# Two leftover output tiles taken as a pair through seven half products, and the ending's order dealt anew

## The chip, the cores and the metric

The kernel runs on one core of a Trainium2 chip. A core has several engines with instruction queues of their own: TensorE (PE; its weight loads are the row PEld) multiplies matrices into PSUM, VectorE (DVE) and ScalarE (ACT) read PSUM and write on-chip memory (SBUF), GpSimd (POOL) here mostly issues loads, and SyncE (SP) issues the stores and the DMA transposes. Sixteen DMA engines move the data. The metric is the device time of one execution in microseconds.

## The reference

Inputs are q, k, v of shape (8, 12, 448, 64) and four weights. Cut to what matters:

```python
scores = q @ k.T / sqrt(64) - log(448)          # per batch and head
x = sigmoid(scores) @ v                          # -> (8, 448, 768), heads side by side
h = relu(x.T @ w_tok1) @ w_tok2                  # mixing over tokens, 448 -> 256 -> 448
u = x + h.T
out = u + relu(u @ w_ch1) @ w_ch2                # mixing over channels, 768 -> 1536 -> 768
```

Output is (8, 448, 768) in float32. The kernel computes in float16 with float32 sums in PSUM.

## The kernel before, in words

One batch is a lot (0 to 7). A lot has three units of four heads each. The work of a unit is a cycle: `qk` (scores and sigmoid, seven pieces), `av` (product with v, result in xT), a DMA transpose to xn (`xtrans_dma`), `tok1` (first token product, ReLU on ScalarE into h1), `ytrans` (second token product, added to xT by VectorE, giving ut). A lot then goes through the channel mixing: `utrans` transposes u by DMA into un, `sevens` computes the hidden layer h2 (448 tokens x 1536), and the second product turns h2 into output rows in tiles of 128 tokens: tiles 0, 1 and 2, and a last piece of 64.

Two of the products use the seven-multiplication scheme of Strassen and Winograd in place of eight. `sevens` does so for the first channel product (L499 is its matmul), with `token_sums` making sums of ut halves on VectorE ahead of it. `ch2_seven` does so for the second product of tiles 0 and 1 of a lot: the two tiles are the two block rows, the low and high half of the 1536 hidden columns the block columns. A half product (`plain`, matmul L763) is six matmuls of 128x128 by 128x384. `sums` makes four sums of h2 blocks on VectorE (L751), and `end` adds each product's PSUM result to the output tile (L781). Products 1, 6, 7, 4 accumulate in one bank (chain X); 2 is chain Y; 5 and 3 are chain Z:

```python
CHAIN = {1: "X", 6: "X", 7: "X", 4: "X", 2: "Y", 5: "Z", 3: "Z"}
```

Tile 2 has no partner and takes the plain way, `ch2` (L549): two halves of 384 output columns, twelve matmuls each. The last 64 tokens of lot 6 go through `last_split` (L631) and those of lot 7 through `ch2_last` (L802, L813).

The order is written out by hand: each engine runs its instructions in the order in which the program names them, and a queue does not go past an instruction that waits. PSUM has eight banks: four named `m0` to `m3` (chosen with `at_bank`) and two tiles of two banks each with the tag `qk`, which the scores use and, in the ending, `av`, `last_split` and `sevens`. `at_bank[0] = Y` with Y = 0, and X = 2.

The ending comes after the loop over cycles: the last `av` and the last transposes of lot 7, the second product of lot 6 laid between them so that TensorE has work while the transposes, ReLUs and sums of lot 7 go on, then `sevens(7)`, then lot 7's second product and its last piece. `store` issues two DMAs per tile on SP (L585). The last piece is copied and stored by VectorE with SP and by ScalarE with its own queue (L823, L825, L834).

Of the kernel before, what the change touches and what calls it, by code (L numbers as in the profile page):

```python
# [9 lines left out]
FP16 = mybir.dt.float16  # L10
# [13 lines left out]
NU = 3  # L24
# [6 lines left out]
def kernel(  # L31
# [53 lines left out]
    def bank(shape, dtype, name):  # L85

        if opening_banks:
            n = opening_banks.pop(0)
        else:
            n = at_bank[0]  # L90
            at_bank[0] = (n + 1) % 4
        return pp.tile(shape, dtype, tag=f"m{n}", bufs=1, name=name)
# [146 lines left out]
    def xtrans_dma(b, u):  # L239
        nc.sync.dma_start_transpose(  # L240
            out=xn_tile(b, u).rearrange("s g t d -> s (g t) d"),
            in_=xTs[b % 2][:, u, :, :].rearrange("d g s -> d (g s)"),
        )
# [38 lines left out]
    def tok1(b, u, relu_on_vector=False, with_scores=False):  # L282

        if not with_scores:
            h1_tile(b, u)
            one = bank([128, 2, 2, 128], FP32, f"tk_{b}_{u}")
            tks[b] = [one[:, tcb, :, :] for tcb in range(2)]
        ps = tks[b]
        for tcb in range(2):
            cols = slice(128 * tcb, 128 * tcb + 128)  # L290
            for t in range(3 if with_scores else 4):
                rows = slice(0, 64 if t == 3 and N_FIRST <= NU * b + u < N_CYCLES - 2 else 128)
                nc.tensor.matmul(  # L293
                    out=ps[tcb],
                    lhsT=w1[rows, t, cols],
                    rhs=xn[b, u][rows, :, t, :],
                    start=(t == 0 and not with_scores),
                    stop=(t == (2 if with_scores else 3)),
                )
        for tcb in range(2):  # L300
            dst, src = h1[b, u][:, tcb, :, :], ps[tcb]
            if relu_on_vector:
                nc.vector.tensor_scalar(
                    out=dst, in0=src, scalar1=0.0, scalar2=None, op0=MAX
                )
            else:
                nc.scalar.activation(out=dst, in_=src, func=RELU)  # L307

    def ytrans(b, u, banks=()):
        for g in range(2):  # L310
            db = NU * g + u
            if banks:
                at_bank[0] = banks[g]
            ps = bank([128, 512], FP32, f"yt_{b}_{db}")
            for tcb in range(2):
                nc.tensor.matmul(  # L316
                    out=ps[:, 0:S],
                    lhsT=h1[b, u][:, tcb, g, :],
                    rhs=w2[:, tcb, :, :],
                    start=(tcb == 0),  # L320
                    stop=(tcb == 1),
                )
            nc.vector.tensor_tensor(  # L323
                out=uts[b % 2][:, db, 0:S], in0=xTs[b % 2][:, u, g, 0:S], in1=ps[:, 0:S], op=ADD
            )


    def utrans(b):
        if b < B - 1:
            nc.vector.tensor_copy(  # L330
                out=uts[b % 2][:, 0:NU, S:512], in_=uts[b % 2][:, NU:NDB, S - 64 : S]
            )
        un[b] = pa.tile([128, NDB, 4, 128], FP16, tag="un", bufs=2, name=f"un_{b}")
        nc.sync.dma_start_transpose(
            out=un[b].rearrange("s db t d -> s (db t) d"),
            in_=uts[b % 2].rearrange("d db s -> d (db s)"),
        )
# [203 lines left out]
    def ch2(b, t, half, n0=0, n1=NCB):  # L541
        cols = slice(DH * half, DH * half + DH)
        if n0 == 0:
            if half == 0:
                outs[b, t] = pa.tile([128, D], FP32, tag="outs", bufs=3, name=f"o_{b}_{t}")
            acc[b] = bank([128, 512], FP32, f"c2_{b}_{t}_{half}")
        ps = acc[b]
        for cb in range(n0, n1):
            nc.tensor.matmul(  # L549
                out=ps[:, 0:DH],  # L550
                lhsT=h2[b][:, BY_GROUP[cb], 128 * t : 128 * t + 128],
                rhs=c2[:, BY_GROUP[cb], cols],
                start=(cb == 0),
                stop=(cb == NCB - 1 and b in un),
            )
        if n1 < NCB:
            return
        if b not in un:
            for n in range(NU):
                nc.tensor.matmul(  # L560
                    out=ps[:, 128 * n : 128 * n + 128],
                    lhsT=uts[b % 2][:, NU * half + n, 128 * t : 128 * t + 128],
                    rhs=ident[:, :],
                    start=False,
                    stop=(n == NU - 1),
                )
        ch2_out(b, t, half, ps)
# [147 lines left out]
    class ch2_seven:  # L715

        CHAIN = {1: "X", 6: "X", 7: "X", 4: "X", 2: "Y", 5: "Z", 3: "Z"}

        def __init__(self, b, X, Y, Z):
            self.b, self.ps, self.banks = b, {}, {"X": X, "Y": Y, "Z": Z}  # L720
            hid = pa.tile(
                [128, 3, NCB // 2, 128], FP16, tag="tr_k", bufs=2, name=f"hid_{b}"
            )
            hid3 = pa.tile([128, NCB // 2, 128], FP16, tag="tr_q", bufs=2, name=f"hid3_{b}")
            self.held = {n: hid[:, at, :, :] for at, n in enumerate((5, 6, 7))}
            self.held[3] = hid3[:, :, :]
            h = h2[b]
            t0, t1 = slice(0, 128), slice(128, 256)
            self.a11, self.a12 = h[:, LOW, t0], h[:, HIGH, t0]
            self.a21, self.a22 = h[:, LOW, t1], h[:, HIGH, t1]  # L730
            self.weights = {1: self.a11, 2: self.a12, 4: self.a22}
            self.moving = {
                1: c2[:, LOW, D1],
                2: c2[:, HIGH, D1],
                3: c2[:, HIGH, D2],
                5: hsums[0],
                6: hsums[1],
                7: hsums[2],
                4: hsums[3],
            }  # L740
# [12 lines left out]
        def begin(self, n):  # L753
            chain = self.CHAIN[n]
            if n in (1, 2, 5):
                at_bank[0] = self.banks[chain]
                self.ps[chain] = bank([128, 512], FP32, f"c8_{self.b}_{n}")
            return self.ps[chain]

        def plain(self, n, k0=0, k1=NCB // 2):  # L760
# [11 lines left out]
                self.end(n)  # L772

        def end(self, n):
            b = self.b
            t, half = {1: (0, 0), 2: (0, 0), 6: (0, 1), 3: (0, 1)}.get(n, (1, int(n != 4)))
            if (b, t) not in outs:
                outs[b, t] = pa.tile([128, D], FP32, tag="outs", bufs=3, name=f"o_{b}_{t}")
            o = outs[b, t][:, DH * half : DH * half + DH].rearrange("s (u d) -> s u d", d=128)
            opens = n in (1, 6, 5, 4)  # L780
            nc.vector.tensor_tensor(  # L781
                out=o,
                in0=un[b][:, NU * half : NU * half + NU, t, :] if opens else o,
                in1=self.ps[self.CHAIN[n]][:, 0:DH].rearrange("s (u d) -> s u d", d=128),
                op=ADD,
            )
            if n in (3, 4):
                store(b, t)
# [485 lines left out]

    lot = B - 2
    before, ahead = divmod(N_CYCLES - 1, NU), divmod(N_CYCLES - 2, NU)
    seven = ch2_seven(lot, X, X + 1, X + 1)
    av(*before, banks=two_banks("xa_end"))
    steps, last_end = last_split(lot, two_banks("c2_end"))
    for f in steps:  # L1280
        f()
    seven.sums(0, 2)

    def halves(b, t, half):
        return [lambda n=n: ch2(b, t, half, n, n + 6) for n in (0, 6)]

    first, second = halves(lot, 2, 0), halves(lot, 2, 1)
    xtrans_dma(*before)
    seven.plain(1)
    seven.plain(2)  # L1290
    seven.sums(2, 4)
    seven.plain(6)
    seven.plain(5)
    last_end()
    at_bank[0] = Y
    tok1(*ahead)
    seven.plain(7)
    seven.plain(3)
    at_bank[0] = Y
    ytrans(*ahead)  # L1300
    token_sums(B - 1, 0, 2)
    seven.plain(4)
    at_bank[0] = X + 1
    first[0]()
    at_bank[0] = Y
    tok1(*before)
    first[1]()
    at_bank[0] = Y
    ytrans(*before)
    at_bank[0] = X  # L1310
    second[0]()
    second[1]()
    token_sums(B - 1, 2, NU)
    utrans(B - 1)
    sevens(B - 1)
    seven = ch2_seven(B - 1, Y + 1, Y, X)
    first, second = halves(B - 1, 2, 0), halves(B - 1, 2, 1)
    seven.plain(1)
    seven.sums(0, 4)
    seven.plain(2)  # L1320
    at_bank[0] = X + 1
    for f in first:
        f()
    seven.plain(5)
    seven.plain(6)
    at_bank[0] = Y
    second[0]()
    seven.plain(3)
    seven.plain(7)
    second[1]()  # L1330
    seven.plain(4)
    at_bank[0] = X
    for w, f in pieces_last(B - 1):
        f()

# [29 lines left out]
```

## Time and profile before

| | us |
|---|---|
| median of 3 runs | 345.11 (344.12 to 345.49) |
| the profiled execution | 343.85 |
| its span, first to last instruction | 341.9 |
| TensorE busy | 334.7 (98%) |
| VectorE busy | 216.7 (63%) |
| ScalarE busy | 212.5 (62%) |
| last TensorE work ends, from the span's start | 337.6 |

Times inside a profile are counted from the span's start. A row of the chain of work or of the timeline gives a start, a length, an engine, a line of the kernel, the tensors (output, then inputs) and a count. SPq and ACTq are the instruction queues that issue DMAs. In a group's row, the numbers after the bar are busy time and mean nanoseconds of one, then the idle time ahead of it and what ended that.

### The profile page before, as it was taken

To read this page: it belongs to the slowest core of one execution; us is meant where nothing else is said; L and a number is where in the kernel's file an instruction comes from. 1 tells how busy PE (TensorE), PEld (TensorE's weight loads), DVE (VectorE), ACT (ScalarE), POOL (GpSimd) and SP (SyncE) were. 2 spreads that over 40 slices of the span, in tenths; PEclk is the share of its full clock that TensorE was granted. 3 is DMA by queue.
4 is the path that set the end of the run, shared out by engine and by line. 5 is a ranking of instruction groups with operands and counts; after the bars stand their busy time and mean duration, and the time that the engine had idled before them with its cause. 6 is when DMAs were issued, how large, how long until landed. Compare 5 with 4: busy or idle time off the path is not lost.

```text
span 341.9 us, 10439 instructions
## 1 busy us (share of the span) xinstructions
PE 334.7 (98%) x4549; PEld 238.8 (70%) x4549; DVE 216.7 (63%) x438; ACT 212.5 (62%) x271; POOL 56.6 (17%) x98
## 2 busy tenths in 40 slices
PE   7999999999999999999999999999999999999994
PEld 4655566555886679766886679766896669768952
DVE  3376467588674775566574584666765685886662
ACT  4996846588658684877648785777648885102400
POOL 8992440040040004000130004000100000000000
PEclk9999999999999999999999999999999999999999
DMA  7999999999999799999999599948991438035406
GB/s 125 172 180 191 207 204 200 169 175 223 219 172 208 119 175 175 209 168 134 191 188 167 123 196 184 223 98 149 199 157 33 102 78 141 5 69 130 86 0 161
DMA packets 104380, 52.17 MB, mean 153 GB/s; under 512 B 76432, under 2 KB 101264, under 8 KB 104336
## 3 DMA queue, kind: packets, MB, share of 16 engines
q1 hardware_dynamic: 78944, 29.70, 47.8%
q0 software_dynamic: 25168, 21.50, 41.7%
q8 instruction: 35, 0.57, 0.7%
q10 hardware_dynamic: 224, 0.33, 0.3%
q14 instruction: 9, 0.07, 0.1%
HBM read 43.45 MB, written 11.01 MB: 159 GB/s over the span
## 4 chain that ended last, share of the span: by engine, by line
PE 90%; ACT 5%; DMA 1%; DVE 1%; issue 1%; ACTq 0%; DVEq 0%
PE c_ab L499 14%; PE qk L184 10%; PE c L549 9%; PE c_c L499 8%; PE c L375 8%; PE xa L215 8%; PE c L631 6%; PE tk L293 5%; PE yt L316 5%; ACT att L191 5%; PE c L763 4%; PE c L613 4%; PE c L352 3%; DMA first_q<-in_q_dram 1%; PE c L802 1%; PE c_a L499 1%
## 5 line engine op out<-in xcount | busy, mean ns | idle before, releaser
L191 ACT ACTIVATE att<-qk,att_bias 128x896 f16<-128x896 f32 x168 | 157.0, 1015 | 41.5 <-PE qk L184 41.1
L184 PE MATMUL qk<-tr_q,tr_k 64*64 64x448 f16 x672 | 57.5, 356 | 0.5 <-DVE tr_k L176 0.2
L499 PEld LDWEIGHTS <-c 128*128 128x128 f16 x504 | 48.4, 98 | 1.1 <-issue 0.3
L224 DVE CAST xT<-xa 128x448 f16<-128x448 f32 x46 | 26.6, 620 | 29.8 <-PE xa L215 29.8
L215 PE MATMUL xa<-att,raw_v 64*64 64x448 f16 x644 | 38.0, 349 | 0.0
L499 PEld LDWEIGHTS <-sum 128*128 128x128 f16 x378 | 36.3, 98 | 0.0
L184 PEld LDWEIGHTS <-tr_k 64*64 64x64 f16 x672 | 20.3, 105 | 19.7 <-issue 12.0
L572 DVE TENSOR_TENSOR o<-un,c 128x384 f32<-128x384 f16 x34 | 18.8, 554 | 23.3 <-PE c L613 10.2
L549 PE MATMUL c<-c,h 128*128 128x384 f16 x180 | 32.9, 326 | 0.0
L375 PE MATMUL c<-c,h 64*64 64x384 f16 x640 | 31.1, 322 | 0.0
L520 ACT ACTIVATE pt_ab<-c_ab 128x896 f32<-128x896 f32 x21 | 19.3, 917 | 16.9 <-PE c_ab L499 16.3
L323 DVE TENSOR_TENSOR ut<-xT,yt 128x448 f16<-128x448 f16 x48 | 27.5, 614 | 1.9 <-PE yt L316 1.9
L215 PEld LDWEIGHTS <-raw_v 64*64 64x64 f16 x672 | 20.3, 107 | 10.9 <-issue 0.4
L1039 POOL COPY gate<-tr_q 128x2 f16<-128x2 f16 x6 | 1.2, 195 | 154.0 <-DMA tr_q<-rel_q 154.0
L549 PEld LDWEIGHTS <-h 128*128 128x128 f16 x180 | 17.2, 98 | 11.3 <-issue 1.0
L307 ACT ACTIVATE h<-tk 128x256 f16<-128x256 f32 x42 | 14.2, 405 | 16.7 <-PE tk L293 16.7
L375 PEld LDWEIGHTS <-h 64*64 64x64 f16 x640 | 18.7, 107 | 7.9
L316 PE MATMUL yt<-w,h 128*128 128x448 f16 x96 | 22.1, 353 | 0.0
L631 PE MATMUL c<-c,h 64*64 64x384 f16 x480 | 22.1, 322 | 0.0
L522 ACT ACTIVATE h<-c_ab 128x896 f16<-128x896 f32 x7 | 6.4, 917 | 24.4 <-PE c_ab L499 24.4
L293 PE MATMUL tk<-xn,w 128*128 128x256 f16 x156 | 21.2, 274 | 0.1
L529 DVE TENSOR_TENSOR h<-pt_ab,c_ab 128x896 f16<-128x896 f32 x14 | 15.2, 1084 | 9.4 <-PE c_ab L499 9.4
(110 smaller groups left out, 473.3 us busy)
## 6 DMA issues: line engine op xcount, KB each, us to landing
out_dram<-o SPq DMA_DIRECT2D x48, 192.0 KB, 3.5
c<-in_moe_w_ch_dram POOLq DMA_DIRECT2D x4, 1152.0 KB, 15.6
raw_k<-in_k_dram POOLq DMA_DIRECT2D x10, 336.0 KB, 9.3
raw_q<-in_q_dram POOLq DMA_DIRECT2D x10, 336.0 KB, 13.3
raw_v<-in_v_dram POOLq DMA_DIRECT2D x10, 336.0 KB, 10.8
out_dram<-o SPq DMA_DIRECT2D x15, 96.0 KB, 2.2
raw_q<-in_q_dram POOLq DMA_DIRECT2D x12, 112.0 KB, 4.9
raw_k<-in_k_dram POOLq DMA_DIRECT2D x12, 112.0 KB, 4.8
```

The lines of the kernel that those rows point to most:

```text
L184: nc.tensor.matmul(out=ps[64 * g : 64 * g + 64, hi, 0:S], lhsT=tr[b, "k"][64 * hi : 64 * hi + 64, u, j, 64 * g : 64 * g + 64], rhs=tr[b, " ...
L191: nc.scalar.activation(out=att[b, u, j][:, :, :], in_=ps[:, :, 0:S], func=SIGMOID, bias=bias_t[:, :], scale=att_scale,)
L215: nc.tensor.matmul(out=ps[g][64 * hi : 64 * hi + 64, 0:S], lhsT=raw[b, "v"][64 * g : 64 * g + 64, u, hi, j, :], rhs=att[b, u, j][64 * g : ...
L224: nc.vector.tensor_copy(out=xTs[b % 2][:, u, g, 0:S], in_=ps[g][:, 0:S])
L293: nc.tensor.matmul(out=ps[tcb], lhsT=w1[rows, t, cols], rhs=xn[b, u][rows, :, t, :], start=(t == 0 and not with_scores), stop=(t == (2 if ...
L316: nc.tensor.matmul(out=ps[:, 0:S], lhsT=h1[b, u][:, tcb, g, :], rhs=w2[:, tcb, :, :], start=(tcb == 0), stop=(tcb == 1),)
L323: nc.vector.tensor_tensor(out=uts[b % 2][:, db, 0:S], in0=xTs[b % 2][:, u, g, 0:S], in1=ps[:, 0:S], op=ADD)
L375: nc.tensor.matmul(out=ps[p][m : m + 64, 0:n], lhsT=lhsT(p, part, m), rhs=rhs(p, part), start=(first and turn == 0), stop=(last and turn = ...
L499: nc.tensor.matmul(out=ps[:, g, p, :], lhsT=weights[n][:, d, 128 * cb : 128 * cb + 128], rhs=moving[n][:, d, :], start=(n in (1, 5, 2) and ...
L520: nc.scalar.activation(out=shaped(part[:, :, :]), in_=ps, func=COPYF)
L549: nc.tensor.matmul(out=ps[:, 0:DH], lhsT=h2[b][:, BY_GROUP[cb], 128 * t : 128 * t + 128], rhs=c2[:, BY_GROUP[cb], cols], start=(cb == 0), ...
L631: nc.tensor.matmul(out=ps[r][m : m + 64, 0:DH], lhsT=lhsT(part, n, m), rhs=rhs(part, n, m), start=(n == 0), stop=(n == n_cb - 1),)
```

## The change

Tile 2 of lot 6 and tile 2 of lot 7 become the two block rows of one more `ch2_seven`, named `both`. Lot 6's hidden layer is in a buffer that `sevens(7)` overwrites, so ScalarE copies its tile 2 to a buffer of its own (`held`) early in the ending. `ch2_seven` takes its rows and its h2 blocks as arguments. The output tile of lot 7's tile 2 goes to a buffer that held v, as the three output buffers are in use. In `both` and in lot 7's `seven`, chains Y and Z share a bank.

`ytrans` in the ending gets a two-bank tile and issues its four matmuls together, then its two adds. The order ahead of `sevens(7)` is dealt anew: `last_end` and both `tok1` come earlier, `token_sums` is done whole, `utrans` comes right behind the second `ytrans`. Behind `sevens(7)` the products of `both` and of `seven` alternate.

```diff
-    def ytrans(b, u, banks=()):
-        for g in range(2):
-            db = NU * g + u
-            if banks:
-                at_bank[0] = banks[g]
-            ps = bank([128, 512], FP32, f"yt_{b}_{db}")
+    def ytrans(b, u, banks=None):
+        def products(g, ps):
             for tcb in range(2):
                 nc.tensor.matmul(
...
+        def add(g, ps):
+            db = NU * g + u
             nc.vector.tensor_tensor(
                 out=uts[b % 2][:, db, 0:S], in0=xTs[b % 2][:, u, g, 0:S], in1=ps[:, 0:S], op=ADD
             )
+        for g in range(2):
+            ps = banks[g] if banks else bank([128, 512], FP32, f"yt_{b}_{NU * g + u}")
+            products(g, ps)
+            if not banks:
+                add(g, ps)
+        for g in range(2 if banks else 0):
+            add(g, banks[g])
...
-        def __init__(self, b, X, Y, Z):
-            self.b, self.ps, self.banks = b, {}, {"X": X, "Y": Y, "Z": Z}
+        def __init__(self, rows, sides, X, Y, Z):
+            self.rows, self.ps, self.banks = rows, {}, {"X": X, "Y": Y, "Z": Z}
...
-            h = h2[b]
-            t0, t1 = slice(0, 128), slice(128, 256)
-            self.a11, self.a12 = h[:, LOW, t0], h[:, HIGH, t0]
-            self.a21, self.a22 = h[:, LOW, t1], h[:, HIGH, t1]
+            (self.a11, self.a12), (self.a21, self.a22) = [
+                (side[:, LOW, :], side[:, HIGH, :]) for side in sides
+            ]
...
-    seven = ch2_seven(lot, X, X + 1, X + 1)
+    seven = ch2_seven(
+        [(lot, 0), (lot, 1)], [tokens(h2[lot], t) for t in range(2)], X, X + 1, X + 1
+    )
     av(*before, banks=two_banks("xa_end"))
     steps, last_end = last_split(lot, two_banks("c2_end"))
     for f in steps:
         f()
+    held = pa.tile([128, NCB, 128], FP16, tag="raw_v", bufs=2, name="held")
+    nc.scalar.activation(out=held[:, :, :], in_=tokens(h2[lot], 2), func=COPYF)
     seven.sums(0, 2)
...
-    first, second = halves(lot, 2, 0), halves(lot, 2, 1)
     xtrans_dma(*before)
+    last_end()
     seven.plain(1)
     seven.plain(2)
     seven.sums(2, 4)
+    at_bank[0] = Y
+    tok1(*ahead)
+    seven.plain(6)
+    at_bank[0] = Y + 1
+    tok1(*before)
+    ytrans(*ahead, banks=two_banks("yt_end_1"))
+    seven.plain(5)
+    ytrans(*before, banks=two_banks("yt_end_2"))
+    utrans(B - 1)
+    seven.plain(7)
+    token_sums(B - 1)
+    seven.plain(3)
+    seven.plain(4)
+    sevens(B - 1)
+    outs[B - 1, 2] = pa.tile([128, D], FP32, tag="raw_v", bufs=2, name=f"o_{B - 1}_2")
+    both = ch2_seven(
+        [(lot, 2), (B - 1, 2)], [held, tokens(h2[B - 1], 2)], Y, Y + 1, Y + 1
+    )
+    seven = ch2_seven(
+        [(B - 1, 0), (B - 1, 1)], [tokens(h2[B - 1], t) for t in range(2)], X + 1, X, X
+    )
+    both.plain(1)
+    seven.sums(0, 2)
+    both.plain(2)
+    seven.plain(1)
+    seven.plain(2)
+    both.sums(0, 2)
     seven.plain(6)
     seven.plain(5)
-    last_end()
-    at_bank[0] = Y
-    tok1(*ahead)
+    seven.sums(2, 4)
+    both.plain(6)
+    both.plain(5)
+    both.sums(2, 4)
     seven.plain(7)
     seven.plain(3)
-    at_bank[0] = Y
-    ytrans(*ahead)
-    token_sums(B - 1, 0, 2)
+    both.plain(7)
+    both.plain(3)
     seven.plain(4)
-    at_bank[0] = X + 1
-    first[0]()
-    at_bank[0] = Y
-    tok1(*before)
-    first[1]()
-    at_bank[0] = Y
-    ytrans(*before)
-    at_bank[0] = X
-    second[0]()
-    second[1]()
-    token_sums(B - 1, 2, NU)
-    utrans(B - 1)
-    sevens(B - 1)
-    seven = ch2_seven(B - 1, Y + 1, Y, X)
-    first, second = halves(B - 1, 2, 0), halves(B - 1, 2, 1)
-    seven.plain(1)
-    seven.sums(0, 4)
-    seven.plain(2)
-    at_bank[0] = X + 1
-    for f in first:
-        f()
-    seven.plain(5)
-    seven.plain(6)
-    at_bank[0] = Y
-    second[0]()
-    seven.plain(3)
-    seven.plain(7)
-    second[1]()
-    seven.plain(4)
-    at_bank[0] = X
+    both.plain(4)
+    at_bank[0] = Y + 1
     for w, f in pieces_last(B - 1):
         f()
```

More of the change, by code (lines that the diff above doesn't have):

```diff
@@ L717 @@
         CHAIN = {1: "X", 6: "X", 7: "X", 4: "X", 2: "Y", 5: "Z", 3: "Z"}
-        def __init__(self, b, X, Y, Z):
-            self.b, self.ps, self.banks = b, {}, {"X": X, "Y": Y, "Z": Z}
+        def __init__(self, rows, sides, X, Y, Z):
+            self.rows, self.ps, self.banks = rows, {}, {"X": X, "Y": Y, "Z": Z}
+            b = rows[1][0]
             hid = pa.tile(
@@ L756, in begin @@
                 at_bank[0] = self.banks[chain]
-                self.ps[chain] = bank([128, 512], FP32, f"c8_{self.b}_{n}")
+                b, t = self.rows[1]
+                self.ps[chain] = bank([128, 512], FP32, f"c8_{b}_{t}_{n}")
             return self.ps[chain]
@@ L774, in end @@
         def end(self, n):
-            b = self.b
-            t, half = {1: (0, 0), 2: (0, 0), 6: (0, 1), 3: (0, 1)}.get(n, (1, int(n != 4)))
+            row, half = {1: (0, 0), 2: (0, 0), 6: (0, 1), 3: (0, 1)}.get(n, (1, int(n != 4)))
+            b, t = self.rows[row]
             if (b, t) not in outs:
@@ L1276, with tokens @@
     before, ahead = divmod(N_CYCLES - 1, NU), divmod(N_CYCLES - 2, NU)
-    seven = ch2_seven(lot, X, X + 1, X + 1)
+    def tokens(side, t):
+        return side[:, :, 128 * t : 128 * t + 128]
+    seven = ch2_seven(
+        [(lot, 0), (lot, 1)], [tokens(h2[lot], t) for t in range(2)], X, X + 1, X + 1
+    )
     av(*before, banks=two_banks("xa_end"))
@@ L1281 @@
         f()
+    held = pa.tile([128, NCB, 128], FP16, tag="raw_v", bufs=2, name="held")
+    nc.scalar.activation(out=held[:, :, :], in_=tokens(h2[lot], 2), func=COPYF)
     seven.sums(0, 2)
-    def halves(b, t, half):
-        return [lambda n=n: ch2(b, t, half, n, n + 6) for n in (0, 6)]
-    first, second = halves(lot, 2, 0), halves(lot, 2, 1)
     xtrans_dma(*before)
+    last_end()
     seven.plain(1)
```

## The prediction

> **What bounds the kernel now.** I read the page first: the engines' shares and the forty slices.
>
> ```profile
> span 341.9 us, 10439 instructions
> ...
> PE 334.7 (98%) x4549; PEld 238.8 (70%) x4549; DVE 216.7 (63%) x438; ACT 212.5 (62%) x271; POOL 56.6 (17%) x98
> ...
> PE   7999999999999999999999999999999999999994
> ```
>
> TensorE is busy in 98% of the span and in every slice but the first and the last. A change of the ending therefore pays by the TensorE time it removes, unless it makes TensorE wait or lengthens what follows its last matmul. Next comes the chain of work that ended last, in order of time, from 295 us on (start, length, engine, output, line, count).
>
> ```profile
> 298.43 4.01 PE c L763 x24
> ...
> 307.96 0.87 PE tk L293 x8
> 308.84 0.97 PE c L549 x6
> 309.81 0.76 PE yt L316 x4
> 310.57 1.95 PE c L549 x12
> 312.52 1.15 PE c_ab L499 x12
> ...
> 314.82 0.57 PE c_c L499 x6
> 315.39 2.30 PE c_ab L499 x24
> ...
> 324.59 1.95 PE c L763 x12
> ...
> 335.32 2.07 PE c L802 x24
> 337.39 0.21 PE c L813 x6
> 337.60 0.54 DVE o L825
> ```
>
> Where rows adjoin, each piece starts within 0.01 us of the end of the one before: the ending is a string of matmuls without holes. The half products of the `ch2_seven` class (L763) and the plain ones (L549) cost the same: 1.95/12 = 0.1625 us for one matmul, 0.975 us for six. I call six of them a block. `tok1` is 0.87, a `ytrans` 0.76 (its two y products). After TensorE's last row, 4.3 us of the span (341.9 less 337.6) are the last copy and stores.
>
> **The change part by part.** *Fewer matmuls.* Tile 2 of lots 6 and 7 now takes 4 halves of 12 matmuls, 48. As a pair through seven half products it takes 7 x 6 = 42. Six matmuls go: 6 x 0.1625 = -0.98 us, all on the path. `tok1`, `ytrans`, the seven products of ch1 and the last pieces keep their counts.
>
> *The order ahead of the seven products of ch1.* The 24 matmuls of lot 6's tile 2 leave this stretch, so the first L499 matmul comes at 312.52 - 24 x 0.1625 = 308.62. From 298.43 the blocks now run: products 1 and 2, `tok1` of the earlier unit, product 6, `tok1` of the later unit at 298.43 + 3 x 0.975 + 0.87 = 302.23, `ytrans` at 303.10, product 5, `ytrans` at 304.83, products 7, 3, 4. What it leans on stands in these rows: SP's queue, landings of the xn transposes from 250 us on and over the whole run, landing of the un transposes, then ACT's and VectorE's groups.
>
> ```profile
> 297.82 1.23 SPq L240 DMA_TRANSPOSE xn<-xT  x1
> ...
> 314.30 4.28 SPq L334 DMA_TRANSPOSE un<-ut  x1
> ```
>
> ```profile
> DMA to landing us min/median/max: 3.0/3.1/3.2
> ```
>
> ```profile
> DMA to landing us min/median/max: 3.0/3.4/11.3
> ```
>
> ```profile
> DMA to landing us min/median/max: 5.9/9.6/11.8
> ```
>
> ```profile
> L520 ACT ACTIVATE pt_ab<-c_ab 128x896 f32<-128x896 f32 x3 | 2.8, 917 | 5.0 <-PE c_ab L499 5.0
> L307 ACT ACTIVATE h<-tk 128x256 f16<-128x256 f32 x4 | 1.3, 380 | 13.4 <-PE tk L293 13.4
> ```
>
> ```profile
> L323 DVE TENSOR_TENSOR ut<-xT,yt 128x448 f16<-128x448 f16 x4 | 2.3, 614 | 0.0
> ```
>
> - The later unit's transposed xn lands about 297.82 + 3.1 = 300.9. `tok1` reads it at 302.23 instead of 307.96: 1.3 us of slack remain of 7.0. Price: nothing. The stores of `last_end`, now issued earlier, stand behind this transpose on SP, not ahead of it.
> - ReLU to `ytrans`: ACT's two ReLUs take at most 0.76. The first pair begins at 301.25 and is needed at 303.10; the second at 303.10, needed at 304.83. Before, the second pair had only the 308.84 block (0.97) as cover and no hole shows, so 1.73 is enough: nothing.
> - The y sums: VectorE starts the last two at 305.6 at the latest and ends by 305.6 + 2 x 0.61 = 306.8; the first L499 needs them at 308.62. `token_sums`, now whole, is four operations of 672 columns. The 768-column sums below take up to 0.58 from start to start, so at most 2.3 us; with the add of product 7 ahead of them (0.56) they end by 306.8 + 0.56 + 2.3 = 309.7. Their first reader, 6ab, starts 2.87 us after 1ab (315.39 less 312.52), at 311.5. Nothing. The adds of products 3 and 4 wait behind them and end near 310.8; bank 2, which product 4 holds, is wanted by 1c at 308.62 + 2.30 = 310.92. This is the thinnest place, about 0.1 us on upper prices. With only 0.47 us pitch for independent operations it is 0.5; I take zero, upper bound 0.3.
> - The un transpose moves ahead, to about 306.8, past the stores of tiles 0 and 1, which now wait behind its 4.28 us issue. They go out from about 311.1 on, and their buffers are wanted again after 320.69. At the longest landing, 11.8 us, un is there by 318.6; the first add that reads un of lot 7 comes after 320.7. Nothing.
> - The held copy is one ACT operation of 1,536 columns, a form that the trace lacks. Two L520 operations cover 1,792 columns in 1.83 us, so that is its bound. ACT ran its last work for lot 6 near 295, and the copy's first reader starts at 320.7: nothing. Even without cover it would cost 1.83.
>
> *The new ending.* The seven products of ch1 end at 324.59 - 3.90 = 320.69; I call this zero. Then come fourteen blocks (84 matmuls, where 42 + 24 stood) and the last pieces. VectorE has 14 adds and 8 weight sums; its rows for this stretch:
>
> ```profile
> 325.61 0.56 DVE L781 TENSOR_TENSOR o<-un,c 128x384 f32<-128x384 f16 x1 [0.31 <-PE c L763]
> 326.08 0.55 DVE L751 TENSOR_TENSOR hid<-h 128x768 f16<-128x768 f16 x1
> 326.66 0.56 DVE L751 TENSOR_TENSOR hid<-hid,h 128x768 f16<-128x768 f16 x1
> ```
>
> Starts are 0.47 us apart, 0.58 where an operation reads the one before; an add starts 0.05 after its block (325.61 against 324.59 + 0.975). So VectorE needs at most 22 x 0.58 = 12.8 us in 14 x 0.975 = 13.65: not the bound, but close. In order: add pair-1 ends at 1.58, sums 5 and 6 by 2.62, pair-2 by 3.09, seven-1 by 3.56, seven-2 by 4.50, the pair's sums 5 and 6 by 5.55. Needed: seven-6 at 3.90 (seven-1 read, slack 0.34), seven-5 at 4.88 (same bank as seven-2, slack 0.38), pair-6 at 5.85 (its sum, slack 0.30). Later slacks are larger: seven-7 at 7.80 wants a sum that is done by 6.96. Price zero; at the three thin places up to 0.2 us each, so 0 to 0.6.
>
> *The stores.* Before, three tiles are stored near the end, now four. The rows are SP's queue and the DMA share by stretch (last two numbers: share of the 16 engines, GB/s).
>
> ```profile
> 333.01 4.35 SPq L585 DMA_DIRECT2D out_dram<-o  x6
> 338.17 0.47 SPq L834 DMA_DIRECT2D out_dram<-o  x1
> ```
>
> ```profile
> 334.00:335.50 1.50, 1.50 (x13) 0.79 (x12) 0.70 (x2) 0.00 (x0) 0.00 (x0) 1.00 0.92 234
> 335.50:336.00 0.50, 0.50 (x10) 0.35 (x8) 0.41 (x1) 0.00 (x0) 0.00 (x0) 1.00 0.39 86
> 336.00:339.00 3.00, 1.56 (x24) 1.00 (x20) 0.55 (x1) 0.48 (x1) 0.00 (x0) 1.00 0.96 252
> 339.00:340.50 1.50, 0.00 (x0) 0.00 (x0) 0.00 (x0) 0.00 (x0) 0.00 (x0) 1.00 0.54 152
> ```
>
> The engines are full from 336 to 339. A tile is 128 x 768 x 4 bytes, 393 KB: 1.56 us at 252 GB/s. Data starts about 1.0 us after the issue (333.01, 334.0). Let E be the end of TensorE (337.60). The last tile's add ends at E - 1.68 in both kernels (2.28 of last pieces, 0.05 and 0.55). Before, tiles were ready at E - 4.6, -2.66 and -1.68; after, at E - 5.58, -3.63, -2.66 and -1.68. With 1.56 each, the third of the four starts moving at E - 1.07 and the fourth ends at E + 2.05. The last stores (197 KB, 0.78 us) are issued at E + 0.57, could move at E + 1.57, and wait for that: end E + 2.83. The same arithmetic for before gives 1.57 + 0.78 = E + 2.35. Cost 0.48, taken as +0.45; bounds 0 (all in time) and 1.56 (one whole tile later).
>
> The Trainium skill, page "DMA: Bandwidth & Descriptors", section Bandwidth, holds that HBM transfers are bound near 358 GB/s per core. By it, as an estimate, a tile would take 1.1 us, the stores would keep up, and the sum would be -0.98. The trace disagrees: 252 GB/s at a share of 0.96.
>
> *Sum.* -0.98 + 0.45 = -0.53 us. The profiled execution took 343.85 us (span 341.9 and 1.95 around it), so it would come to 343.3. The median of the runs shown, 345.11, is 1.26 above that execution; against it I predict 344.6.
>
> **The rivals.** *Stores hidden.* The last stores land as soon after E as before, because the fourth tile's data slips into holes like 335.5 to 336.0 (share 0.39). For it: that hole. Against: 0.96 after it. Time 345.11 - 0.98 = 344.1.
>
> *VectorE's hand-offs eat the gain.* Both classes put products 2 and 5 in one bank, and product 6 follows the add of 1 in its bank, with slacks of 0.30 to 0.38. If each of the three comes 0.5 late, and 1c by 0.3, TensorE loses 0.2 + 0.2 + 0.1 + 0.3 = 0.8: time about 345.4. Against: VectorE's starts are regular, and 0.58 for every operation still fits. The Trainium skill, "PSUM — Partial Sum Buffer", section Summary, speaks for it: what reads a result while matmuls run should have another bank than they write. The order here meets that by waits, and no run yet shows whether they bite.
>
> *The xn transpose comes too late: slower.* Its slack falls to 1.3 us. Place: the second `tok1`, 302.23. Every microsecond of landing beyond 4.4 holds TensorE for one. It passes 0.5% slower, 1.73 us, at 4.4 + 0.53 + 1.73 = 6.7 us of landing; at 7 us the time is 344.6 + 2.6 = 347.2. For: 11.3 us was the longest in the run. Against: after 250 us it is 3.0 to 3.2, with the loads gone.
>
> **How the numbers follow.** About 0.5% (1.7 us) is what this kernel's measurement tells from no change; its runs lie 344.12 to 345.49. Forecast 0.58; stores hidden 0.16; hand-offs 0.10; xn late 0.06; another wait above 2.3 us that I did not find 0.04; more than 0.5% faster, for which no row offers a mechanism, 0.06. The first three lie within 0.5%: 0.84. Slower 0.10, faster 0.06. The range is the first three with the spread of the runs: 343.3 to 346.0; the forecast's own is 343.8 to 345.2.
>
> **What would show it.** 48 plain L549 matmuls gone and 42 half products of L763 in their place; the chain in the ending still without holes; the span from the first L499 matmul of the last lot to E longer by 18 matmuls, 2.92 us, and what leads there shorter by 3.90; between E and the last landing 0.45 us more, with a share near 0.96 from E - 2.6 on. I am wrong if TensorE waits on xn before `tok1`, on VectorE at 1c, or in the first six blocks of the new ending.

## The result and the profile after

The changed kernel takes 344.08 us (median; 342.71 to 345.09) against 345.12 for the kernel before: ratio 0.9966, 95% interval 0.9951 to 0.9981, a gain of 0.66 to 1.69 us. The prediction said 344.6, within 0.5% of no change, range 343.3 to 346.0.

The profiled execution took 344.08 us with a span of 342.3. That span is 0.4 longer than the one before, although the kernel is faster. One span can't tell, since the unchanged part ahead of the ending varies by more than the change is worth (the profiled execution of e12_last_add took 347.98 us where its median is 344.04). So I measure the ending alone, from the first matmul of the last `av` to the end of the span. These are rows of the chain of work that ended last, in order of time; first the one row of the kernel before that the prediction did not show, then the changed kernel.

```profile
295.03 1.45 PE xa_end L215 x28
```

```profile
296.38 1.45 PE xa_end L215 x28
...
299.77 2.06 PE c L772 x12
...
302.70 0.97 PE c L772 x6
303.68 0.87 PE tk L293 x8
...
307.04 2.93 PE c L772 x18
309.97 1.15 PE c_ab L507 x12
...
312.26 0.57 PE c_c L507 x6
...
322.04 13.65 PE c L772 x84
...
337.97 0.54 DVE o L834
```

TensorE's part of the ending runs from the `xa_end` row to the last copy: 42.57 us before (337.60 less 295.03), 41.59 after. That is 0.98 less. The row of 84 half products lasts 13.65 = 84 x 0.1625, so the new ending has no hole. The tail from there to the end of the span is 4.30 before (341.9 less 337.60) and 4.33 after. The whole ending went from 46.87 to 45.92.

The last thing to land is ScalarE's store of its half of the last piece. These are its issue and its time to landing, before the change:

```profile
338.14 0.54 ACTq L834 DMA_DIRECT2D out_dram<-o  x1
```

```profile
out_dram<-o ACTq DMA_DIRECT2D x1, 96.0 KB, 2.4
```

and after it:

```profile
338.51 0.54 ACTq L843 DMA_DIRECT2D out_dram<-o  x1
```

```profile
out_dram<-o ACTq DMA_DIRECT2D x1, 96.0 KB, 2.7
```

It is issued 0.54 us after TensorE's end in both. To the hundredth the trace has its landing 2.96 after TensorE's end before the change and 3.26 after it: 0.30 later. The tail hardly shows this, because the stretch from that landing to the end of the span is 1.36 before and 1.05 after. At its end SP waits for the stores' semaphores (the counters by which a DMA reports its landing), one behind the other in a fixed order, about 0.06 us each. Before the change ScalarE's last store reports to the second in this order (number 107), and seven more waits come behind it. In the changed kernel it reports to the last one (118); SP's own last store (113) holds SP until 341.07, and when SP comes to 118, at 341.37, that store has landed. These rows are the eight waits from 107 on before the change, and the six from 113 on after it (how many, length in ns, first and last start):

```profile
L1360 SPq EVENT_SEMAPHORE  x8: 27/28/28, 340.6 to 341.0; - x8
```

```profile
L1372 SPq EVENT_SEMAPHORE  x6: 28/28/28, 341.1 to 341.4; - x6
```

Two engines and a queue that the prediction leaned on, from the timeline of the changed kernel:

```profile
296.36 1.48 ACT L1298 ACTIVATE held<-h 128x1536 f16<-128x1536 f16 x1 [0.15 <-DVE h L540]
```

```profile
311.00 0.55 DVE L790 TENSOR_TENSOR o<-un,c 128x384 f32<-128x384 f16 x1
```

```profile
299.17 1.23 SPq L240 DMA_TRANSPOSE xn<-xT  x1
...
308.26 4.21 SPq L342 DMA_TRANSPOSE un<-ut  x1
```

The held copy takes 1.48 us while nobody waits for it. Product 4's add ends at 311.55; 1c, which wants its bank, starts at 312.26. The stores, by stretch (last two numbers: share of the DMA engines, GB/s):

```profile
336.00:339.00 3.00, 1.93 (x28) 1.28 (x24) 0.83 (x2) 0.49 (x1) 0.00 (x0) 1.00 0.95 271
338.00:340.00 2.00, 0.00 (x0) 0.00 (x0) 0.51 (x1) 0.48 (x1) 0.00 (x0) 1.00 0.90 305
```

From 338 to 340 the changed kernel moves 305 GB/s, more than the 252 on which the prediction reckoned.

### The profile page after: what moved, and what is told of

Read it like the earlier page. It is cut to its first block, busy times and chain, and to the rows that moved or that the text cites. A ratio compares the mean times of both kernels' runs of the same rounds, so it can differ in the third digit from the quotient of the medians.

```text
span 342.3 us, 10437 instructions
## 1 busy us (share of the span) xinstructions
PE 335.2 (98%) x4543; PEld 238.9 (70%) x4543; DVE 219.1 (64%) x441; ACT 214.3 (63%) x272; POOL 56.7 (17%) x98
## 4 chain that ended last, share of the span: by engine, by line
PE 91%; ACT 5%; DMA 1%; DVE 1%; issue 1%; ACTq 0%; DVEq 0%
PE c_ab L507 14%; PE qk L184 10%; PE c_c L507 8%; PE c L383 8%; PE xa L215 8%; PE c L557 6%; PE c L772 6%; PE c L639 6%; PE tk L293 5%; PE yt L313 5%; ACT att L191 5%; PE c L621 4%; PE c L360 3%; DMA first_q<-in_q_dram 1%; PE c L811 1%; PE c_a L507 1%
## 5 line engine op out<-in xcount | busy, mean ns | idle before, releaser
L580 DVE TENSOR_TENSOR o<-un,c 128x384 f32<-128x384 f16 x30 | 16.6, 554 | 20.8 <-PE c L621 10.2
L323 DVE TENSOR_TENSOR ut<-xT,yt 128x448 f16<-128x448 f16 x44 | 25.2, 614 | 1.7 <-PE yt L313 1.7
L383 PEld LDWEIGHTS <-h 64*64 64x64 f16 x640 | 18.7, 107 | 7.9
L557 PE MATMUL c<-c,h 128*128 128x384 f16 x132 | 24.1, 326 | 0.0
L537 DVE TENSOR_TENSOR h<-pt_c,c_c 128x448 f16<-128x448 f32 x21 | 12.9, 616 | 12.6 <-PE c_c L507 12.6
L313 PE MATMUL yt<-w,h 128*128 128x448 f16 x88 | 20.3, 353 | 0.0
L639 PEld LDWEIGHTS <-h 64*64 64x64 f16 x528 | 15.4, 107 | 6.7
```

Source lines behind the costliest of these rows:

```text
L313: nc.tensor.matmul(out=ps[:, 0:S], lhsT=h1[b, u][:, tcb, g, :], rhs=w2[:, tcb, :, :], start=(tcb == 0), stop=(tcb == 1),)
L323: nc.vector.tensor_tensor(out=uts[b % 2][:, db, 0:S], in0=xTs[b % 2][:, u, g, 0:S], in1=ps[:, 0:S], op=ADD)
L383: nc.tensor.matmul(out=ps[p][m : m + 64, 0:n], lhsT=lhsT(p, part, m), rhs=rhs(p, part), start=(first and turn == 0), stop=(last and turn = ...
L537: nc.vector.tensor_tensor(out=shaped(dst), in0=shaped(parts[gs, which]), in1=ps, op=ADD)
L557: nc.tensor.matmul(out=ps[:, 0:DH], lhsT=h2[b][:, BY_GROUP[cb], 128 * t : 128 * t + 128], rhs=c2[:, BY_GROUP[cb], cols], start=(cb == 0), ...
L639: nc.tensor.matmul(out=ps[r][m : m + 64, 0:DH], lhsT=lhsT(part, n, m), rhs=rhs(part, n, m), start=(n == 0), stop=(n == n_cb - 1),)
```

## The experiments

Edits are against the changed kernel. Lengths are in us. "TensorE" is TensorE's part of the ending, and the tail is what follows it. "Landing" is the time from TensorE's end to the landing of the last store; it is a part of the tail. A span is shown to 0.1 us, so up to 0.05 of a tail or an ending is rounding. A ratio is to the kernel before, with its 95% interval.

| run | TensorE | tail | landing | ending | time, ratio |
|---|---|---|---|---|---|
| before | 42.57 | 4.30 | 2.96 | 46.87 | 345.12 |
| after | 41.59 | 4.33 | 3.26 | 45.92 | 344.08, 0.9966 |
| e0_after_again | 41.60 | 4.42 | 3.34 | 46.02 | 343.17 (one run) |
| e1_eight | 42.58 | 4.29 | 2.94 | 46.87 | 344.78, 1.0005 (0.9987 to 1.0024) |
| e2_no_store | 41.60 | 4.12 | 3.05 | 45.72 | 343.67, 0.9969 (0.9943 to 0.9996) |
| e3_late_store | 41.60 | 5.77 | 4.53 | 47.37 | 345.14, 1.0015 (1.0001 to 1.0029) |
| e4_tok_early | 43.19 | 4.42 | 3.41 | 47.61 | 345.59, 1.0026 (1.0002 to 1.0051) |
| e5_two_sums | 42.66 | 4.34 | 3.34 | 47.00 | 344.94, 0.9997 (0.9979 to 1.0015) |
| e6_old_order | 42.62 | 4.37 | 3.37 | 46.99 | 344.71, 0.9986 (0.9973 to 0.9999) |
| e7_spread | 41.60 | 4.35 | 3.01 | 45.95 | 343.72, 0.9960 (0.9940 to 0.9980) |
| e8_spread_halves | 41.60 | 4.19 | 2.96 | 45.79 | 343.82, 0.9942 (0.9911 to 0.9974) |
| e10_late_two_queues | 41.60 | 4.68 | 3.35 | 46.28 | 345.64 (one run) |
| e11_two_queues | 41.60 | 4.27 | 2.97 | 45.87 | 343.90, 0.9959 (0.9925 to 0.9992) |
| e12_last_add | 41.59 | 4.52 | 3.46 | 46.11 | 344.04, 0.9959 (0.9932 to 0.9987) |

**The ruler.** The changed kernel itself, unedited.

> The changed kernel once more, to see how far the lengths read from one profile repeat. The ending, from the first matmul of the last av to the end of the span, was 46.87 us before (341.9 less 295.03) and 45.92 us after (342.3 less 296.38); what follows TensorE's last matmul was 4.30 and 4.33 us. Every theory expects 45.9 within 0.15 and 4.3 within 0.15; a larger spread would make the endings useless as a ruler.

TensorE's part repeats within 0.01 us, the tail within 0.09 and the landing within 0.08. Three edits further down leave the last stores as they are (e4_tok_early, e5_two_sums, e6_old_order); with them the landing lies between 3.26 and 3.41. So holes on TensorE can be read to a hundredth of a microsecond, but differences of the tail below 0.1 and of the landing below 0.15 can't be told.

**Is the gain the six matmuls?** The pair by eight half products. `eighth` makes six matmuls of the plain way; R6 is lot 6's tile 2.

```diff
-    both.plain(1)
+    eighth(R6, 0, Y, 0, 6)
     seven.sums(0, 2)
-    both.plain(2)
+    eighth(R6, 0, Y, 6, NCB)
...
```

> The pair of tiles through eight half products in place of seven (48 matmuls, 4 adds and no pair sums on VectorE), all else as changed, the stores at the same places. Theory that the gain is the six matmuls alone: TensorE's part of the ending is 0.98 us longer than after (42.57 us, as before the change), the time is 1.0 us above the changed kernel, 345.1. Rival, that the gain came from the new order or from elsewhere: ending as after, 344.1.

TensorE 42.58, 0.99 more than after and what it was before. With the six matmuls back the time, too, can't be told from that of the kernel before. On TensorE the gain is the six matmuls and, to 0.01 us, nothing else.

**What do the stores cost?** Four runs. First, one store less, and one more held back to the end.

```diff
-            if n in (3, 4):
+            if n in (3, 4) and (b, t) != (B - 2, 2):
                 store(b, t)
```

In e3_late_store the tile is `(B - 2, 1)`, and `store(lot, 1)` stands behind `seven.plain(3)`.

> The store of lot 6's tile 2 is left out (128 output rows stay unwritten), all else as changed. Theory of the prediction, that the fourth tile costs the last stores 0.45 us at 252 GB/s: what follows TensorE's last matmul falls from 4.33 to 3.9 us. Rival, stores hidden: it stays within 0.1 of 4.3, as before the change, when three tiles were stored there.

> The store of lot 6's tile 1 is held back until just ahead of that of lot 6's tile 2, so that five tiles are stored near the end (lot 7's tile 1 gets another buffer for it). At 252 GB/s (1.56 us a tile) the arithmetic of the prediction gives the last stores 1.17 us later than with four tiles: 5.5 us after TensorE's last matmul. At 284 GB/s, what the engines moved in the changed kernel from 336.5 to 340.5, it gives 1.38 us a tile and 0.75 later: 5.0 to 5.1. Rival, stores hidden as TensorE's last pieces cover them: 4.3 to 4.4.

Without the fourth tile the tail is 4.12, which lies between the two expectations; with the 0.1 of the ruler it speaks for a cost of 0.1 to 0.3, below 0.45. The landing comes at 3.05, 0.2 to 0.3 sooner than in the two profiles of the changed kernel. With a fifth tile the tail is 5.77, above both estimates; the landing comes 1.19 to 1.27 later, near the 1.17 reckoned at 252 GB/s. So the stores crowd the end: a little with four tiles, heavily with five. Then who sets the pace? One of each tile's two stores on ScalarE's queue, with five tiles (e10, shown) and with four (e11, `t in (2,)`):

```diff
         for par in range(2):
-            nc.sync.dma_start(
+            queue = nc.scalar if par and (b == B - 1 or (b == B - 2 and t in (1, 2))) else nc.sync
+            queue.dma_start(
```

> e3_late_store with one of each tile's two stores issued by ScalarE in place of SP. In e3_late_store SP took 6.46 us to issue ten stores and issued its last one 0.42 us late. If SP's issuing sets the 5.77 us tail of that kernel, two queues bring it to 5.3 or less; if the DMA engines do, it stays at 5.6 to 5.9.

> The changed kernel with one of each of the last four tiles' two stores issued by ScalarE. If the engines' rate or SP's queue delayed the last stores, the tail falls from 4.33 to 4.40 us towards 4.2; if they are hidden, it stays within 0.1 of 4.35. The time is that of the changed kernel, 344.1, in both cases within what it can tell.

The tail with five tiles falls from 5.77 to 4.68, though the engines and the bytes are the same. DMA by stretch, with one queue (e3_late_store):

```profile
333.80:336.80 3.00, 2.98 (x35) 1.79 (x33) 0.92 (x2) 0.00 (x0) 0.00 (x0) 1.00 0.86 259
```

and with two (e10_late_two_queues):

```profile
336.20:341.20 5.00, 2.97 (x35) 1.78 (x33) 1.46 (x3) 0.49 (x1) 0.00 (x0) 1.00 0.95 331
```

In this stretch SP's queue alone gives 259 GB/s (267 from 333 to 339), two queues 331 at a share of 0.95. A share of 0.96 with 252 GB/s was therefore not the engines' limit. With stores from one queue the pace was lower over several microseconds, though not in each: from 335 to 336 SP's queue alone moved 347 in e3_late_store. Whether SP's issuing or something in the queue behind it sets this pace, these runs don't separate: in e3_late_store SP's ten issues took 6.46 us and its last one came 0.42 late, but the landings grew too. And in the kernel before, four stores (786 KB) were issued between 334.96 and 336.76; over the 3 us of the prediction's row that is 262 GB/s, so its 252 may be no more than what there was to store.

With four tiles a second queue brings a tail of 4.27, within the ruler of 4.33 to 4.42. The landing, at 2.97, is clear of the ruler: the changed kernel's one queue did delay it. SP issues its fourth tile's two stores 1.13 and 0.53 us ahead of TensorE's end; with two queues both go out 1.66 ahead of it.

**A floor of the tail.** The pair's tiles earlier (e7), and tiles stored in halves on two queues as well (e8).

The new order:

```python
    both.plain(1)
    both.sums(0, 2)
    both.plain(2)
    seven.plain(1)
    both.sums(2, 4)
    both.plain(6)
    seven.sums(0, 2)
    both.plain(5)
    seven.plain(2)
    seven.sums(2, 4)
    both.plain(7)
    both.plain(3)
    seven.plain(6)
    both.plain(4)
    seven.plain(5)
    seven.plain(7)
    seven.plain(3)
    seven.plain(4)
```

> The new ending in another order: the pair's seven products finish by the tenth of the fourteen blocks, so that its two tiles are stored about 7.1 and 5.6 us ahead of TensorE's end and only two tiles in the last 3 us. No hole is expected on TensorE (slacks 0.37 and more). Theory that stores crowd the end: the last landing comes 0.3 us sooner after TensorE's end than in the changed kernel (2.9 in place of 3.2) and the ending is 45.6 to 45.9. Rival, stores hidden: ending as after, 45.9.

> The order of e7_spread, and the tiles of the new ending stored in halves of 384 columns as soon as each half is done, one DMA on SP's queue and one on ScalarE's. Only two halves (393 KB in all) are then released in the last 3 us. Theory that stores crowd the end (252 GB/s, queue to be emptied first): the last data ends 2.3 us after TensorE and the tail, from TensorE's end to the span's end, falls to about 4.0 us. Theory that the tail is the latency of the last two stores alone (copy, issue, landing): 4.3, as before the change, in e1_eight and in e7_spread.

No hole in either (TensorE 41.60). In e7_spread the landing is 3.01, 0.25 to 0.33 sooner than in the changed kernel, as the theory of crowding expects. The tail is 4.35 all the same, as after: the last landing reports to semaphore 107 again, and 1.34 us follow it. In e8_spread_halves the last data ends 2.6 us after TensorE, not 2.3, the landing is 2.96 and the tail 4.19, between the two expectations. Its DMA rows show why the landing can't come sooner; TensorE ends at 337.91 there:

```profile
335.40:338.40 3.00, 2.46 (x32) 1.55 (x30) 1.05 (x2) 0.47 (x1) 0.00 (x0) 1.00 0.76 199
338.40:339.40 1.00, 0.00 (x0) 0.00 (x0) 0.05 (x1) 0.02 (x1) 0.00 (x0) 1.00 0.00 0
339.40:340.40 1.00, 0.00 (x0) 0.00 (x0) 0.00 (x0) 0.00 (x0) 0.00 (x0) 1.00 0.73 194
```

For a whole microsecond the engines stand idle, waiting for the last stores to be copied and issued. About 2.95 us from TensorE's end to the last landing is what the last piece costs by itself; the landings of the kernel before, e1_eight and e11_two_queues lie there, too (in e1_eight the four tiles are stored further apart). The changed kernel lies 0.3 to 0.4 above that. What follows the landing goes with the semaphore in all 14 profiles: 1.34 to 1.36 us where the last store reports to 107 (before, e1, e7), 1.27 to 1.29 for 108 (e8, e10, e11), 1.23 for 113 (e3), 1.12 for 117 (e2), 1.03 to 1.06 for 118 (the other six). No run changed the semaphore alone.

**The wait for xn.** The second `tok1` moved up.

```diff
     seven.plain(1)
+    at_bank[0] = Y + 1
+    tok1(*before)
     seven.plain(2)
...
     seven.plain(6)
-    at_bank[0] = Y + 1
-    tok1(*before)
```

> The second tok1 is moved ahead, to right behind product 1 of lot 6. In the changed kernel its xn transpose is issued at 299.17 and product 1 ends at 300.80; with 3.1 us of landing xn is there at 302.27. Theory of the prediction, that xn lands 3.1 us after its issue and that a late xn holds TensorE for just as long: a hole of 1.4 to 1.6 us ahead of that tok1 and an ending longer by the same, about 47.4 us; time 1.5 above the changed kernel. Rival, that xn is there much sooner (its DMA shows no more data 2.6 us after the issue): a hole of 1.0 or less.

The chain of e4_tok_early:

```profile
297.74 1.34 PE c_end L639 x33
299.09 3.06 DMA xn<-xT
302.14 0.05 issue
302.19 1.05 PE tk L293 x8
```

The chain now runs through the transpose: 3.06 us from its issue to its landing, and TensorE's part is 1.60 longer. The first expectation holds: a late xn costs TensorE its lateness, one for one.

**VectorE's thin places.** Two sums made twice.

```diff
     both.plain(1)
     seven.sums(0, 2)
+    seven.sums(0, 2)
```

> VectorE makes the first two sums of lot 7's tiles twice, 1.05 us of extra work in the new ending just ahead of the thin places. Theory of the prediction, slack 0.34 at product 6 of lot 7: TensorE waits about 0.7 there, once, as VectorE gains slack from the wait; ending 46.6 us. Rival, that VectorE with 11 busy us of 13.65 takes this without effect: no hole, ending 45.9.

A wait as forecast, but 1.07 in place of 0.7. The chain of e5_two_sums:

```profile
321.36 0.99 PE c L772 x6
...
322.85 0.56 DVE hid L759
...
323.43 0.57 DVE hid L759
...
324.03 0.57 DVE hid L759
...
325.10 1.02 DVE o L790 x2
326.12 0.04 issue
326.16 9.91 PE c L772 x60
```

Product 6 of lot 7 could start at 321.36 + 4 x 0.975 = 325.26 and starts at 326.16: a hole of 0.90. Each of the repeated sums touches what the one before wrote, so they start 0.58 to 0.60 apart, and the two of them cost 1.2 rather than 1.05; less the slack, that leaves 0.9. The row of 60 matmuls lasts 9.91 where 9.75 is due, so another 0.16 is lost further on.

**Seven products without the new order.** The order ahead of `sevens(7)` as before the change, less lot 6's tile 2.

```diff
...
+    seven.plain(4)
+    at_bank[0] = Y
+    tok1(*before)
+    at_bank[0] = Y
+    ytrans(*before)
+    token_sums(B - 1, 2, NU)
+    utrans(B - 1)
     sevens(B - 1)
```

> Seven half products alone: the pair and the new ending as changed, but the order ahead of the seven products of ch1 as before the change, without lot 6's tile 2 that lay in it as filling. Theory that the new order is needed to keep TensorE fed: a hole of 0.4 to 0.8 us between the second tok1 and its ytrans (ReLU with no cover) and one of 0.2 to 0.6 ahead of the first matmul of ch1; ending 46.6 to 47.3 us, which eats the gain of 0.98. Rival, that the order is worth nothing: 45.9.

The chain of e6_old_order:

```profile
308.17 0.89 PE tk L293 x8
309.06 0.02 issue
309.08 0.67 ACT h L307 x2
309.75 0.04 issue
309.79 0.92 PE yt L313 x4
310.71 1.26 PE c_ab L507 x12
```

TensorE waits 0.73 us for ScalarE's ReLUs (309.06 to 309.79), then loses 0.16 in `ytrans` (0.92 for 0.76) and 0.11 in 1ab (1.26 for 1.15), with smaller losses beside: 1.03 in all, as much as the six matmuls bring. Tile 2 of lot 6 had been the cover of those waits. Once it moves, the new order is what keeps the gain.

**A further step that gave nothing.** The last 64 tokens' u added by VectorE in place of identity matmuls.

```diff
-        if b < B - 1:
-            nc.vector.tensor_copy(
-                out=uts[b % 2][:, 0:NU, S:512], in_=uts[b % 2][:, NU:NDB, S - 64 : S]
-            )
+        nc.vector.tensor_copy(
+            out=uts[b % 2][:, 0:NU, S:512], in_=uts[b % 2][:, NU:NDB, S - 64 : S]
+        )
...
-        add_on_pe = final or b not in un
+        add_on_pe = b not in un
...
```

> The changed kernel, with u added to the last 64 tokens of lot 7 by one VectorE add from the transposed un, as the other tiles have it, in place of six small identity matmuls (0.21 us on the path) and two copies on VectorE and ScalarE; the un transpose gets a small copy ahead of it on VectorE. Theory that TensorE's matmuls and nothing else set the ending: TensorE's part is 0.21 us shorter (41.4), the tail as before it or up to 0.1 longer (an add of 0.55 for copies of 0.55 and 0.49, both stores behind it), ending 45.7 to 45.8, time 343.9. Rival, that the copy ahead of the un transpose or the one add costs as much: 45.9 or more.

The six matmuls of 0.21 us are gone, but TensorE's part stays at 41.59. The chain of e12_last_add shows where they went:

```profile
310.75 1.95 PE c L771 x12
312.70 0.01 issue
312.71 1.14 PE c L771 x6
```

Product 4 of lot 6 takes 1.14 in place of 0.975. The copy ahead of the un transpose stands ahead of product 7's add on VectorE, and product 4 accumulates in the bank which that add reads. In the changed kernel that add ends at 308.70 and product 4's first matmul starts at 308.83, so the slack there is 0.13. The rival expectation was right. A copy placed elsewhere was not tried.

None of the versions meant to be faster (e7, e8, e11, e12) is told from the changed kernel by its time. By its ending, e8_spread_halves is the shortest of them, by 0.13 us, hardly more than the ruler can tell.

## Why the prediction was right, point by point

- *Six matmuls, -0.98 us, all on the path.* Right to the hundredth: TensorE's part 41.59 for 42.57, and 42.58 with eight products. From the first matmul of ch1 to TensorE's end it is 28.00 for 25.08, 2.92 longer, and what leads there is 13.59 for 17.49, 3.90 shorter, as forecast.
- *The order ahead costs nothing.* Right: the chain has no wait there. The second `tok1` starts 7.30 us after the first `av` matmul (303.68 less 296.38); forecast were 7.20. The 0.1 is a gap that I overlooked and that both kernels have, where the first half product follows the small matmuls of `last_split`: 2.06 us for 12 matmuls where 1.95 are due, and 4.01 for 24 before, where 3.90 are due. The slack on xn was 1.4 us (303.68 less the landing at 299.17 + 3.06); I had said 1.3. The held copy took 1.48 within its bound of 1.83. What I called the thinnest place, 1c, had 0.7 to spare, since VectorE's independent operations start 0.47 apart. I overlooked a thinner one of 0.13: product 4 waits for the add of product 7, and e12_last_add met it.
- *The new ending, slacks of 0.30 to 0.38, price zero.* Right: 13.65 us for 84 matmuls. e5_two_sums shows that these slacks are real and no larger than that.
- *The stores, +0.45 us.* The delay was there, and its cost was not. The last landing comes 0.30 to 0.45 us later after TensorE's end (3.26 to 3.41 in the five profiles with these stores, 2.96 before), and stores spread over more time (e7_spread) or over two queues (e11_two_queues) take it back. But the tail grew by only 0.03 to 0.12. The step that failed is one that the prediction did not write down: that what follows the last landing stays as it was. It fell from 1.36 to 1.05, as the last store now reports to the semaphore for which SP waits last. The sum was off too, in its part on the kernel before: it has the last data ending 2.35 us after TensorE before and 2.83 after the change, and the traces have 2.61 and 2.81.
- *The pace.* I took 252 GB/s at a share of 0.96 for what the engines can do. That reading was wrong: two queues bring 331 at 0.95. As a rate, the rule of the Trainium skill that I set aside ("DMA: Bandwidth & Descriptors", section Bandwidth, near 358 GB/s for HBM per core) was nearer; e10_late_two_queues held 331 over 5 us.
- *The rival stores hidden.* Its time, 344.1, is what was measured; I gave it 0.16. Its mechanism, the last landing as soon after TensorE's end as before, is not what happened. That the time met this rival is luck: which semaphore the last store reports to had no part in any of the forecasts.
- *Hand-offs and late xn.* Both mechanisms exist, and e5_two_sums and e4_tok_early show them at their prices; in the changed kernel neither occurs.
- *The sum.* -0.53 forecast; by the endings it is -0.95, by the times -1.04. In parts: -0.98 from the matmuls, +0.30 from the landing, -0.31 from what follows it, and the rounding of the spans. The time fell within the range; most of what it came out below the forecast is the third part.

## What to carry to other kernels

When work leaves a place, ask what it covered there: the six matmuls saved are lost again if the order isn't mended. Where the bound engine has no holes, the length of the ending between two marks in the trace resolves hundredths of a microsecond that times and spans don't. A DMA share near one is no proof of a full rate; a second issuing queue tells whether it is. And where the length of a tail doesn't move, look at its parts: here two of 0.3 us cancelled.

## What was not expected of the hardware

Stores from SP's queue alone moved 252 to 271 GB/s over 3 us or more and those from two queues 331, at shares of 0.86 to 0.96 (the kernel before, e3_late_store, the changed kernel; e10_late_two_queues). VectorE's operations that read or overwrite what the one before wrote start 0.58 to 0.60 us apart where independent ones of the same size start 0.47 apart, which in e5_two_sums was part of the difference between the wait forecast and the one measured. And the last 1.03 to 1.36 us of the span, behind the last landing, depend on where the last store's semaphore stands in the order of SP's waits, by 0.3 us from the second to the last.
